# Query loads by head pair, scatters through disjoint views, and gathers issued ahead of scatters, in a fused retention and mixture-of-experts kernel

## The chip, the cores and the metric

The kernel runs on one core of a Trainium2 chip. The metric is the device time of one execution in microseconds, as a median of several runs. The trace behind all rows is one profiled execution of the same kernel.

## The reference

The inputs q, k and v have 8 batches, 8 heads, 576 positions and 64 values a head. The first half is retention: scores with a causal, exponentially decaying mask and no softmax. The second half is a switch layer over the 4608 rows that come out: each row goes to the one of 8 experts with the largest logit and is scaled by its gate.

```python
scores = scale * np.matmul(q, k.transpose(0, 1, 3, 2))
Dmat = np.where(rel >= 0, gamma[:, None, None] ** rel[None, :, :], 0.0)
x = np.matmul(scores * Dmat[None], v)        # then (B * S, H * D) = (4608, 512)

logits = x @ w_gate                          # 8 experts
expert_idx = np.argmax(logits, axis=1)
for e in range(E):
    mask = expert_idx == e
    h = np.maximum(x[mask] @ w1[e], 0.0)     # 512 -> 1024
    out[mask] = gate_w[mask, None] * (h @ w2[e])
```

## The kernel before, in words

Every engine runs its instructions in the order in which the program writes them; no planner reorders them. Waits between engines and DMAs are set from the tiles, and from the regions of DRAM tensors, that instructions share.

**Attention stage.** The sequence is cut into 40 blocks, five for each batch: four of 128 positions and a last one that holds the remaining 64 queries and 64 keys. The loop over blocks (i, or batch b and block c) does for each: GpSimd scales one head pair of the next batch's queries (`scale_q`, line 219, tile qq from qt) and the keys of block i + 3 (`scale_k`, line 229, kk from kt); TensorE makes scores, transposes keys (psk, copied to kT), updates the state, transposes the block's result back to rows (psr, written to the DRAM tensor `x_rows`), forms the output (psx) and at the end of the block transposes the scaled query pair (`stage_TQ`, psq, copied to qT by ScalarE). SP issues the loads: keys and values of block i + 7, from seven buffers each, the write of `x_rows`, and in block 4 of batch b the whole query of batch b + 2 as one DMA of 1 MB (`load_q`, line 93), into one of two buffers. The four head pairs of batch 0 come as four DMAs at the start, and batch 1 after the first blocks. From block 21 on one 512 KB piece of expert weights is loaded in each block (wst, three staging buffers) and cast to bf16 by VectorE. Routing runs beside the later batches on VectorE.

**Expert stage.** The rows of each expert come in two units: two tiles of 128 rows (phase 0, routed from the first half of the tokens) and three tiles (phase 1). `seq` lists the sixteen units: phase 0 of experts 0 to 2, phase 1 of the same, and then both phases of each expert from 3 on. For a unit `mm1` multiplies by w1 (pm, ReLU on ScalarE into ht), `trans` transposes the gathered rows of the next unit (pt from xg, copied to xt by VectorE), and `mm2` multiplies by w2 (py), scales by the gate on VectorE (ys, four buffers) and scatters the tile to `out` with an indirect DMA of GpSimd (line 755). `gather` (line 603) fetches a unit's rows into xg (six buffers) with one indirect DMA of GpSimd for each tile. The weights of experts 2 to 7 are 48 pieces of 512 KB over six staging buffers: each cast, up to five on VectorE within `mm1` and one on ScalarE after each tile of `mm2`, is followed by the load of another piece.

The gathers of the first three units are issued during the last blocks of attention, and those of units 4 and 5 when the third unit is done, since their slots are known only then. From the fourth unit on the loop issues the gather of unit i + 2 at its end, behind the scatters of unit i:

```python
            if nxt:
                trans(*nxt)
            mm2(e, ph, ht, during2)
        if i >= 3 and i + 2 < len(seq):
            gather(*seq[i + 2])
```

After the last unit a count of overflowing rows is read by all engines (line 814), and a branch (line 816) skips a fallback that nothing here needs.

Of the kernel before, what the change touches and what calls it, by code (L numbers as in the profile page):

```python
# [3 lines left out]

# [9 lines left out]
F32 = mybir.dt.float32  # L14
# [4 lines left out]
P = 128  # L19
B, H, S, DH = 8, 8, 576, 64  # L20
DM = H * DH
E, F = 8, 1024
NP = H // 2
NCH = 4
# [7 lines left out]
CA = 256  # L32
CB = 384
# [5 lines left out]
def kernel(  # L39
# [10 lines left out]
    nc = tc.nc  # L50
# [22 lines left out]
    ldq = p1.enter_context(tc.tile_pool(name="ldq", bufs=2))  # L73
# [11 lines left out]
    NB = len(blocks)  # L85
    qts, kts, vts, qrs = {}, {}, {}, {}

    def load_q(b, first):

        qt = ldq.tile([P, H, NCH, DH], F32, tag="q", name="qt")  # L90
        step = 2 if first else H
        for h in range(0, H, step):
            nc.sync.dma_start(out=qt[:, h:h + step, :, :],
                              in_=q[b, h:h + step, 0:NCH * P, :].rearrange("h (p s) d -> p h s d", p=P))
        qts[b] = qt

    def load_k(i):

        b, c = blocks[i]
        kt = ldk.tile([P, H, DH], F32, tag="k", name="kt")  # L100
        if c < NCH:
            nc.sync.dma_start(out=kt[:, :, :], in_=k[b, :, c * P:(c + 1) * P, :].rearrange("h p d -> p h d"))
        else:
            nc.sync.dma_start(out=kt[0:REM, :, :], in_=q[b, :, NCH * P:S, :].rearrange("h p d -> p h d"))
            nc.sync.dma_start(out=kt[REM:P, :, :], in_=k[b, :, NCH * P:S, :].rearrange("h p d -> p h d"))
        kts[i] = kt

    def load_v(i):

        b, c = blocks[i]  # L110
        vt = ldk.tile([P, H, DH], F32, tag="v", name="vt")
        if c < NCH:
            nc.sync.dma_start(out=vt[:, :, :], in_=v[b, :, c * P:(c + 1) * P, :].rearrange("h p d -> p h d"))
        else:
            for j in range(2):
                nc.sync.dma_start(out=vt[j * REM:(j + 1) * REM, 0:NP, :],
                                  in_=v[b, NP * j:NP * (j + 1), NCH * P:S, :].rearrange("h p d -> p h d"))
        vts[i] = vt

    load_k(0)  # L120
    load_q(0, True)
    load_v(0)
    for i in range(1, 5):
        load_k(i)
        load_v(i)


    ident = consts.tile([P, P], F32, name="ident")
# [73 lines left out]
    def cast_w(eng):  # L202
        e, part, st = staged.pop(0)
        w1b, w2b = wb[e]
        c = part % 4
        if part < 4:
            casts[eng](out=w1b[:, c, :], in_=st[:, :])
        else:
            casts[eng](out=w2b[:, 2 * c:2 * c + 2, :], in_=st[:, :].rearrange("p (s d) -> p s d", d=DM))
# [6 lines left out]
    def scale_q(b, p):  # L216
        h0 = 2 * p
        qq = wkp.tile([P, NCH, P], F32, tag="qq")
        nc.gpsimd.tensor_tensor(  # L219
            out=qq[:, :, :].rearrange("p s (h d) -> p h s d", d=DH), in0=qts[b][:, h0:h0 + 2, :, :],  # L220
            in1=qg[:, 0:NCH, h0:h0 + 2].rearrange("p s h -> p h s").unsqueeze(3)
                .to_broadcast([P, 2, NCH, DH]), op=ALU.mult)
        qqs[(b, p)] = qq

    def scale_k(i):
        if i >= NB:
            return
        kk = wk3.tile([P, H, DH], F32, tag="kk")
        nc.gpsimd.tensor_tensor(out=kk[:, :, :], in0=kts.pop(i)[:, :, :],  # L229
                                in1=kg[:, blocks[i][1], :].unsqueeze(2).to_broadcast([P, H, DH]), op=ALU.mult)  # L230
        kks[i] = kk
# [365 lines left out]
    def gather(e, ph):  # L597
        nb = (CA if ph == 0 else CB) // P
        nr = NTOK // 2 if ph == 0 else NTOK
        for j in range(nb):  # L600
            i = j * E + e
            xg = gp.tile([P, DM], BF16, tag="xg", name="xg")
            nc.gpsimd.indirect_dma_start(  # L603
                out=xg[:, :], out_offset=None, in_=x_rows[0:nr, :],
                in_offset=bass.IndirectOffsetOnAxis(ap=slots[ph][1][:, i:i + 1], axis=0),
                bounds_check=nr - 1, oob_is_err=False)
            gat_t[(e, ph, j)] = xg
# [30 lines left out]
    stage_TK(1)  # L638
    stage_SC(0)
    stage_S(0)  # L640
    load_q(1, False)
    load_k(5)
    load_v(5)
    load_k(6)
# [6 lines left out]
    for i, (b, c) in enumerate(blocks):  # L651
        if c < NP and b + 1 < B:
            scale_q(b + 1, c)
        scale_k(i + 3)
        stage_SC(i + 1)
        stage_TK(i + 2)
        stage_S(i + 1)
        if i > 0:
            stage_R(i - 1)
        if c == 0 and b > 0:  # L660
            stage_L1(b - 1)
        stage_AV(i)
        if i + 7 < NB:
            load_k(i + 7)
            load_v(i + 7)
        if c == 4 and b + 2 < B:
            load_q(b + 2, False)
        if c < NP and b + 1 < B:
            stage_TQ(b + 1, c)
        if c == 0 and b > 0:  # L670
            stage_L2(b - 1)
        if i >= first_early and nearly < len(early):
            load_w(*early[nearly], stpool)
            nearly += 1
        if len(staged) > 2 or (i == NB - 1):
            while len(staged) > (2 if i < NB - 1 else 0):
                cast_w("V")
        if (b, c) == (B // 2, 1):
            rf = route_first()
        if rf is not None:  # L680
            steps(rf, 5)
        if i == NB - 5:
            while steps(rf, 1):
                pass
            gather(0, 0)
            gather(1, 0)
            gather(2, 0)
# [16 lines left out]
    psH = p2.enter_context(tc.tile_pool(name="psH", bufs=3, space=PSUM))  # L704
    psY = p2.enter_context(tc.tile_pool(name="psY", bufs=3, space=PSUM))

    seq = [(e, 0) for e in range(3)] + [(e, 1) for e in range(3)] + [(e, ph) for e in range(3, E) for ph in (0, 1)]
    xts = {}
    wq = [(e, i) for e in range(2, E) for i in range(8)]
# [6 lines left out]
    def trans(e, ph):  # L716
        nb = (CA if ph == 0 else CB) // P
        xt = xtp.tile([P, NPT, nb * P], BF16, tag=f"xt{ph}", name="xt")
        for j in range(nb):
            xg = gat_t.pop((e, ph, j))  # L720
            pt = psT.tile([P, NPT, P], BF16, tag="pt")
            for c in range(NPT):
                tr(pt[:, c, :], xg[:, c * P:(c + 1) * P], identb[:, :])
            nc.vector.tensor_copy(out=xt[:, :, j * P:(j + 1) * P], in_=pt[:, :, :])  # L724
        xts[(e, ph)] = xt
# [18 lines left out]
    def mm2(e, ph, ht, between):  # L744
        nb = (CA if ph == 0 else CB) // P
        w1b, w2b = wb[e]
        tids, tidg, gat = slots[ph]
        for j in range(nb):
            i = j * E + e
            py = psY.tile([P, DM], F32, tag="py")  # L750
            for fb in range(NFB):
                mm(py[:, :], ht[:, fb, j * P:(j + 1) * P], w2b[:, fb, :], fb == 0, fb == NFB - 1)
            ys = yp.tile([P, DM], F32, tag="ys")
            nc.vector.tensor_scalar(out=ys[:, :], in0=py[:, :], scalar1=gat[:, i:i + 1], scalar2=None, op0=ALU.mult)  # L754
            nc.gpsimd.indirect_dma_start(  # L755
                out=out[:, :], out_offset=bass.IndirectOffsetOnAxis(ap=tids[:, i:i + 1], axis=0),
                in_=ys[:, :], in_offset=None, bounds_check=NTOK - 1, oob_is_err=False)
            between()

# [12 lines left out]
    for i, (e, ph) in enumerate(seq):  # L772
        nxt = seq[i + 1] if i + 1 < len(seq) else None
        quota = [5]

        def during1():
            if i < 3:
                steps(rr, 6)
            if i >= 1 and quota[0] > 0 and staged and (i >= 2 or len(staged) > 2):
                cast_w("V")  # L780
                fetch(1)
                quota[0] -= 1

        def during2():
            if i < 3:
                steps(rr, 8)
            if staged:
                cast_w("A")
                fetch(1)

        ht = mm1(e, ph, during1)
        if nxt == (0, 1):
            mm2(e, ph, ht, during2)
            while steps(rr, 1):
                pass
            gather(0, 1)
            gather(1, 1)
            trans(*nxt)
        else:
            if nxt:  # L800
                trans(*nxt)
            mm2(e, ph, ht, during2)
        if i >= 3 and i + 2 < len(seq):
            gather(*seq[i + 2])
    p2.close()


# [8 lines left out]
    with tc.If(over > 0):  # L816
        with ExitStack() as p3:
# [24 lines left out]
            for e in range(E):  # L842
# [4 lines left out]
                with tc.For_i(0, NT, 1) as t:  # L847
# [8 lines left out]
                        out=xg[:, :], out_offset=None, in_=x_rows[:, :],  # L856
# [16 lines left out]
                    for fb in range(NFB):  # L873
# [5 lines left out]
                        out=out[:, :], out_offset=bass.IndirectOffsetOnAxis(ap=ci[:, 0:1], axis=0),  # L879
                        in_=ys[:, :], in_offset=None, bounds_check=NTOK - 1, oob_is_err=False)  # L880
# [30 lines left out]
```

## Time and profile before

| | us |
|---|---|
| median of 3 runs | 565.05 |
| lowest and highest run | 563.92, 566.07 |
| profiled execution | 561.75 |
| its span | 560.0 |

| engine | busy us | share of the span |
|---|---|---|
| TensorE, matmuls | 384.8 | 69% |
| TensorE, weight loads | 267.3 | 48% |
| VectorE | 200.6 | 36% |
| ScalarE | 162.9 | 29% |
| GpSimd | 162.7 | 29% |

The span is what the profiler saw from the first to the last instruction; the execution's own time holds 1.75 us more. The mean granted clock of TensorE was 0.841 of full speed. Attention takes the first 265 us or so, the experts the rest. A share of busy time is a mean over both stages, so the stages have to be looked at one by one.

### The profile page before, as it was taken

The page shows a single profiled execution, that of the slowest core. Times are in us where ns is not written, and L with a number is a line of the kernel's source. Part 1 is how long each engine was busy: PE and PEld are TensorE (multiplying, and loading weights), DVE is VectorE, ACT ScalarE, POOL GpSimd, SP SyncE. Part 2 cuts the span into 40 slices and gives each one's busy share as a digit, 9 for nine tenths or more (in the row PEclk, how much of TensorE's full clock was granted, in tenths as well). Part 3 has the DMA queues.
Part 4 walks back from the last instruction along what each step waited for, and adds up shares of the span by engine and source line. Part 5 has one row for each costly group of instructions (what it writes and reads, how often), then busy time and mean ns, then how long its engine had stood idle before and what let it go on. Part 6 is the DMA issues. An engine that isn't in the chain of part 4 may idle for free. (4 is left out here: it accounts for less than half of the span.)

```text
span 560.0 us, 14566 instructions
## 1 busy us (share of the span) xinstructions
PE 384.8 (69%) x6322; PEld 267.3 (48%) x6322; DVE 200.6 (36%) x453; ACT 162.9 (29%) x301; POOL 162.7 (29%) x196
## 2 busy tenths in 40 slices
PE   4695959779696758795684491935786848677660
PEld 3584848567575647674462250413443434344330
DVE  2342323323275755764892340403321211112110
ACT  3252524335251422342332162313210212121020
POOL 8423305060514206240021512124213232422220
PEclk9898998979797997889798596858877878888695
DMA  8956483736488595561768497276111111111110
GB/s 212 231 135 167 99 204 77 194 78 164 116 221 241 127 274 143 156 180 50 266 240 336 137 319 287 94 275 220 57 47 54 58 56 57 67 57 47 61 60 14
DMA packets 112010, 82.33 MB, mean 147 GB/s; under 512 B 83263, under 2 KB 96063, under 8 KB 111937
## 3 DMA queue, kind: packets, MB, share of 16 engines
q1 hardware_dynamic: 106816, 66.61, 41.6%
q0 software_dynamic: 5120, 14.69, 7.6%
q8 instruction: 52, 0.85, 0.7%
q14 instruction: 22, 0.17, 0.1%
HBM read 67.13 MB, written 15.20 MB: 147 GB/s over the span
## 5 line engine op out<-in xcount | busy, mean ns | idle before, releaser
L740 ACT ACTIVATE ht<-pm 128x384 bf16<-128x384 f32 (+1 forms) x96 | 50.5, 526 | 202.7 <-PE pm L57 202.1
L755 POOL DMA_INDIRECT out_dram<-ys,tids x40 | 40.8, 1019 | 216.7 <-DVE ys L754 107.0
L57 PE MATMUL py<-w2b,ht 128*128 128x512 bf16 x320 | 91.1, 452 | 0.0
L57 PE MATMUL pm<-xt,w1b 128*128 128x256 bf16 (+1 forms) x512 | 75.2, 306 | 7.3 <-DVE xt L724 7.3
L60 PE MATMUL pt<-identb,xg 128*128 128x128 bf16 x160 | 20.8, 279 | 83.6 <-DMA xg<-x_rows,tidg 83.0
L219 POOL TENSOR_TENSOR qq<-qt,qg 128x512 f32<-128x512 f32 x32 | 33.8, 1060 | 137.1 <-DMA qt<-in_q_dram 96.1
L57 PEld LDWEIGHTS <-w1b 128*128 128x128 bf16 x512 | 51.1, 100 | 30.9 <-issue 9.6
L724 DVE COPY xt<-pt 128x512 bf16<-128x512 bf16 x40 | 16.6, 422 | 125.6 <-PE pt L60 125.5
L57 PEld LDWEIGHTS <-ht 128*128 128x128 bf16 x320 | 36.2, 115 | 48.6 <-issue 25.4
L60 PEld LDWEIGHTS <-xg 128*128 128x128 bf16 x160 | 12.7, 120 | 92.7 <-DMA xg<-x_rows,tidg 91.6
L754 DVE TENSOR_SCALAR ys<-py,gat 128x512 f32<-128x512 f32 x40 | 30.0, 750 | 65.5 <-PE py L57 65.4
L60 PE MATMUL psq<-ident,qq 128*128 128x128 f32 x128 | 25.6, 335 | 40.5 <-POOL qq L219 40.5
L229 POOL TENSOR_TENSOR kk<-kt,kg 128x512 f32<-128x512 f32 x40 | 43.4, 1092 | 18.5 <-issue 11.6
L603 POOL DMA_INDIRECT xg<-x_rows,tidg x40 | 41.2, 1030 | 12.1 <-issue 9.6
L360 DVE TENSOR_TENSOR xT<-psx,xo 128x512 f32<-128x512 f32 x32 | 22.1, 692 | 51.4 <-ACT xo L352 51.4
L60 PEld LDWEIGHTS psq<-ident,qq 128*128 128x128 f32 x128 | 16.4, 165 | 44.2 <-POOL qq L219 42.8
L60 PE MATMUL psk<-ident,kk 128*128 128x128 f32 x160 | 30.9, 323 | 9.3 <-POOL kk L229 7.0
L251 ACT COPY kT<-psk 128x512 f32<-128x512 f32 x40 | 23.6, 590 | 39.5 <-PE psk L60 39.5
L57 PE MATMUL psx<-qT,so 64*64 64x64 f32 x512 | 32.7, 221 | 1.7 <-issue 1.7
L241 ACT COPY qT<-psq 128x512 f32<-128x512 f32 x32 | 18.9, 590 | 45.5 <-PE psq L60 45.5
L311 DVE TENSOR_TENSOR sc<-pssc,tri 128x512 f32<-128x512 f32 (+1 forms) x40 | 25.2, 630 | 19.0 <-PE pssc L57 19.0
L352 ACT COPY xo<-psx 128x512 f32<-128x512 f32 (+1 forms) x40 | 21.8, 546 | 33.2 <-PE psx L57 33.0
(119 smaller groups left out, 527.4 us busy)
## 6 DMA issues: line engine op xcount, KB each, us to landing
wst<-in_moe_w_dram SPq DMA_DIRECT2D x64, 512.0 KB, 6.2
kt<-in_k_dram SPq DMA_DIRECT2D x32, 256.0 KB, 4.4
vt<-in_v_dram SPq DMA_DIRECT2D x32, 256.0 KB, 4.6
qt<-in_q_dram SPq DMA_DIRECT2D x7, 1024.0 KB, 7.6
x_rows<-xr SPq DMA_DIRECT2D x32, 128.0 KB, 2.4
qt<-in_q_dram SPq DMA_DIRECT2D x4, 256.0 KB, 4.7
kt<-in_q_dram SPq DMA_DIRECT2D x8, 128.0 KB, 2.9
kt<-in_k_dram SPq DMA_DIRECT2D x8, 128.0 KB, 3.1
```

The costliest lines, as they stand in the source:

```text
L57: nc.tensor.matmul(out=out, lhsT=lhsT, rhs=rhs, start=start, stop=stop, skip_group_check=True)
L60: nc.tensor.transpose(out=out, in_=in_, identity=identity)
L219: nc.gpsimd.tensor_tensor(out=qq[:, :, :].rearrange("p s (h d) -> p h s d", d=DH), in0=qts[b][:, h0:h0 + 2, :, :], in1=qg[:, 0:NCH, h0:h0 ...
L229: nc.gpsimd.tensor_tensor(out=kk[:, :, :], in0=kts.pop(i)[:, :, :], in1=kg[:, blocks[i][1], :].unsqueeze(2).to_broadcast([P, H, DH]), op=A ...
L251: nc.scalar.copy(out=kT[:, :, :].rearrange("p a t -> p (a t)"), in_=pst[:, :])
L311: nc.vector.tensor_tensor(out=sc[:, :, 0:n, :], in0=ps[:, :, 0:n * DH].rearrange("p j (a i) -> p j a i", i=DH), in1=tri[:, :].unsqueeze(1) ...
L352: nc.scalar.copy(out=xo[:, :], in_=psx[:, 1, 0:n * P])
L360: nc.vector.tensor_tensor(out=dst, in0=psx[:, 0, 0:n * P], in1=xo[:, :], op=ALU.add)
L603: nc.gpsimd.indirect_dma_start(out=xg[:, :], out_offset=None, in_=x_rows[0:nr, :], in_offset=bass.IndirectOffsetOnAxis(ap=slots[ph][1][:, ...
L740: nc.scalar.activation(out=ht[:, f0:f0 + per, :], in_=pm[:, :, :], func=AF.Relu)
L754: nc.vector.tensor_scalar(out=ys[:, :], in0=py[:, :], scalar1=gat[:, i:i + 1], scalar2=None, op0=ALU.mult)
L755: nc.gpsimd.indirect_dma_start(out=out[:, :], out_offset=bass.IndirectOffsetOnAxis(ap=tids[:, i:i + 1], axis=0), in_=ys[:, :], in_offset=N ...
```

## The change

`load_q` loads one head pair (256 KB) at a time. Batch 1 is loaded in between the first keys and values, and in block c (0 to 3) of batch b the pair c of batch b + 2 is loaded; the load in block 4 is gone. The scatters write through 40 views of `out` that the tracking of dependencies takes as disjoint, one for each scatter. The gather of unit i + 2 is issued between `trans` of unit i + 1 and `mm2` of unit i; the branch for the third unit is as it was, and the gathers of units 4 and 5 with it.

```diff
-    def load_q(b, first):
-
-        qt = ldq.tile([P, H, NCH, DH], F32, tag="q", name="qt")
-        step = 2 if first else H
-        for h in range(0, H, step):
-            nc.sync.dma_start(out=qt[:, h:h + step, :, :],
-                              in_=q[b, h:h + step, 0:NCH * P, :].rearrange("h (p s) d -> p h s d", p=P))
-        qts[b] = qt
+    def load_q(b, p):
+
+        if p == 0:
+            qts[b] = ldq.tile([P, H, NCH, DH], F32, tag="q", name="qt")
+        h = 2 * p
+        nc.sync.dma_start(out=qts[b][:, h:h + 2, :, :],
+                          in_=q[b, h:h + 2, 0:NCH * P, :].rearrange("h (p s) d -> p h s d", p=P))
...
     load_k(0)
-    load_q(0, True)
+    for p in range(NP):
+        load_q(0, p)
     load_v(0)
-    for i in range(1, 5):
+    load_k(1)
+    load_v(1)
+    load_q(1, 0)
+    for i in range(2, 5):
         load_k(i)
         load_v(i)
+        load_q(1, i - 1)
...
     stage_S(0)
-    load_q(1, False)
     load_k(5)
...
-        if c == 4 and b + 2 < B:
-            load_q(b + 2, False)
+        if c < NP and b + 2 < B:
+            load_q(b + 2, c)
...
+    outs = iter(bass_types.dram_disjoint_views(out, E * (CA + CB) // P))
...
             nc.gpsimd.indirect_dma_start(
-                out=out[:, :], out_offset=bass.IndirectOffsetOnAxis(ap=tids[:, i:i + 1], axis=0),
+                out=next(outs)[:, :], out_offset=bass.IndirectOffsetOnAxis(ap=tids[:, i:i + 1], axis=0),
...
             if nxt:
                 trans(*nxt)
+            if i >= 3 and i + 2 < len(seq):
+                gather(*seq[i + 2])
             mm2(e, ph, ht, during2)
-        if i >= 3 and i + 2 < len(seq):
-            gather(*seq[i + 2])
```

## Rows read from the trace of the kernel before

**Rows 1.** Waits of the span: who waited for whom, total us, times, longest.
```profile
PE psq L60 <- POOL qq L219: 40.5, 8, 7.1
PEld L60 <- DMA xg<-x_rows,tidg: 91.6, 30, 13.6
```

**Rows 2.** Timeline, TensorE: start us, us, line, operation, count, [idle before, releaser].
```profile
52.56 1.12 PE L60 MATMUL psq<-ident,qq 128*128 128x128 f32 x4 [5.64 <-POOL qq L219]
...
59.62 0.65 PE L60 MATMUL psq<-ident,qq 128*128 128x128 f32 x4
...
64.19 0.66 PE L60 MATMUL psq<-ident,qq 128*128 128x128 f32 x4
...
83.76 1.12 PE L60 MATMUL psq<-ident,qq 128*128 128x128 f32 x4 [6.59 <-POOL qq L219]
```

**Rows 3.** Timeline, SP's queue, around 45 us.
```profile
44.98 0.57 SPq L93 DMA_DIRECT2D qt<-in_q_dram  x1
```

**Rows 4.** Timeline, GpSimd, the same batch.
```profile
51.45 1.06 POOL L219 TENSOR_TENSOR qq<-qt,qg 128x512 f32<-128x512 f32 x1 [18.03 <-DMA qt<-in_q_dram]
```

**Rows 5.** Timeline, GpSimd, between two units of the expert stage.
```profile
415.90 1.00 POOL L755 DMA_INDIRECT out_dram<-ys,tids  x1 [2.58 <-DMA out_dram<-ys,tids]
419.41 0.98 POOL L755 DMA_INDIRECT out_dram<-ys,tids  x1 [2.51 <-issue]
420.69 1.04 POOL L603 DMA_INDIRECT xg<-x_rows,tidg  x1 [0.30 <-issue]
```

**Rows 6.** Timeline, TensorE, the same units.
```profile
415.36 3.66 PE L57 MATMUL pm<-xt,w1b 128*128 128x256 bf16 x32
...
423.58 0.61 PE L60 MATMUL pt<-identb,xg 128*128 128x128 bf16 x4 [4.57 <-DMA xg<-x_rows,tidg]
...
447.31 3.66 PE L57 MATMUL pm<-xt,w1b 128*128 128x256 bf16 x32
```

**Rows 7.** DMA issues: tensors, queue, count, KB each, median us to landing.
```profile
qt<-in_q_dram SPq DMA_DIRECT2D x7, 1024.0 KB, 7.6
qt<-in_q_dram SPq DMA_DIRECT2D x4, 256.0 KB, 4.7
```

**Rows 8.** Windows: stretch, length, busy per engine, granted clock, DMA share, GB/s.
```profile
51.50:82.60 31.10, 24.44 (x658) 20.38 (x658) 10.13 (x21) 11.98 (x23) 9.18 (x9) 0.88 0.58 141
175.40:210.20 34.80, 24.48 (x658) 20.09 (x658) 21.85 (x51) 11.33 (x23) 10.25 (x9) 0.89 0.75 199
```

**Rows 9.** Windows, a stretch of the expert stage.
```profile
320.00:340.00 20.00, 15.54 (x93) 8.49 (x91) 6.87 (x12) 12.99 (x21) 2.02 (x2) 0.98 0.95 333
```

**Rows 10.** Timeline, TensorE, third and fourth unit.
```profile
292.61 3.66 PE L57 MATMUL pm<-xt,w1b 128*128 128x256 bf16 x32
296.10 3.62 PE L57 MATMUL py<-w2b,ht 128*128 128x512 bf16 x16
...
317.40 6.93 PE L57 MATMUL pm<-xt,w1b 128*128 128x384 bf16 x32 [0.52 <-DVE xt L724]
324.17 0.61 PE L60 MATMUL pt<-identb,xg 128*128 128x128 bf16 x8
...
325.29 5.34 PE L57 MATMUL py<-w2b,ht 128*128 128x512 bf16 x24
...
330.47 5.36 PE L57 MATMUL pm<-xt,w1b 128*128 128x384 bf16 x32
```

**Rows 11.** Chain of waits that ended last: start us, us, what.
```profile
540.74 0.75 DVE ys L754
...
541.80 4.62 DMA out_dram<-ys,tids
```

**Rows 12.** Timeline, all engines, between third and fourth unit.
```profile
299.75 0.75 DVE L754 TENSOR_SCALAR ys<-py,gat 128x512 f32<-128x512 f32 x1 [0.97 <-PE py L57]
...
312.63 1.00 POOL L603 DMA_INDIRECT xg<-x_rows,tidg  x1 [0.30 <-issue]
```

**Rows 13.** The branch's line: operation, durations min/median/max in ns, first and last start.
```profile
L816 PEldq COMPARE_BRANCH  x1: 4076/4076/4076, 542.6 to 542.6; - x1
```

More of the change, by code (lines that the diff above doesn't have):

```diff
@@ L5 @@
 import concourse.bass as bass
+import concourse.bass_types as bass_types
 import concourse.tile as tile
```

## The prediction

> **What bounds the kernel now.** I read the waits of the whole span first, then the timelines of TensorE, SP and GpSimd around the longest of them, then busy time by stretch, then the chain that ended last. TensorE carries the work in both stages, and it stops for two things [rows 1]: 40.5 us in 8 waits for a scaled query tile (psq on qq), and 91.6 us in 30 waits for gathered rows (the weight load's row on xg). What each of them is late for, only the timelines say.
>
> In the attention stage the wait comes once per batch. The reader is to see in [rows 2] a transpose of psq at 52.56 after 5.64 us of idling, at 1.12 us for its four matmuls, and one at 59.62 that took 0.65 us after no wait: the second cost of a stall is a slow block behind it (52.56 to 59.62 is 7.06 us; 59.62 to 64.19, a block of the same kind, is 4.57). The cause stands in [rows 3] and [rows 4]: SP issues the 1 MB query load at 44.98, behind the value load that waits for the block before, and scaling starts at 51.45, as soon as it has landed. The load is issued when its user is next in line.
>
> In the expert stage [rows 5] show the chain. Scatters of one unit go out at 415.90 and 419.41, 3.5 us apart although one takes 1.0 us: each waits until the one before has landed. The gather for the next unit stands behind them at 420.69, and TensorE transposes its rows at 423.58, after 4.57 us of idling [rows 6]. A pair of units takes 415.36 to 447.31, 31.95 us.
>
> **The change, part by part.**
>
> *Query loads.* The 1 MB load per batch becomes four of 256 KB, one per block, each a full batch ahead of its scaling. Lead: five blocks, over 20 us at 4.57 each, against 4.7 us to land [rows 7]. The buffer is that of two batches before, whose last reader ran in the batch before, so SP is not held up by it. SP issues three more loads per batch; it waits for other engines during most of each batch and has room for them. Value: the 40.5 us go. The slow blocks go too: 7.06 less 4.57 less some 0.5 for two transposes of the router in it, 2.0 each; for seven stalls 13.5, the shorter ones costing a little less. Ceiling 54. Late next: the DMA engines. A batch without weights used 0.58 of 31.1 us, 18.0 us of transfers [rows 8], and would now have 31.2 - 6.6 - 2.0 = 22.6 us: 80 per cent. The batch with weights used 0.75 of 34.8, 26.1 us, and at 0.95, the highest share seen [rows 9], needs 27.5 us, where TensorE would need about 26. The loads run seven blocks ahead and smooth that, so I take off 4: **50 us**. Bounds: 0, if the engines were full, and 54. At the start the query pieces of batch 1 go ahead of later keys: each of 256 KB, some 1.3 us at the 199 GB/s of the second row there; the scaling of keys may start that much later, while the query that it waits beside comes earlier.
>
> A rule speaks against the split: the Trainium skill, DMA: Bandwidth & Descriptors, Rules for kernel authors, wants at least 1 MiB in a DMA, and its section on the anatomy of one DMA gives a fixed cost of about 2 us each. By that, 21 more transfers cost an estimated 42 us if nothing covers them, and the forecast below would be some 463. In the rows a 256 KB load takes 4.7 us and a 1 MB load 7.6, so a fixed part is there; what matters is whether it occupies the engines or is only latency, which is the second rival.
>
> *Scatters as disjoint views.* This takes away the wait of a scatter for the one before. No row shows a scatter without it. Nearest above: 3.5 us apart, as now. Nearest below: a gather, 1.0 us of GpSimd and 0.3 between two. I take 1.3, since 1.0 is what the scatter itself takes. What waits next is the ys tile, on four buffers. GpSimd then has ten such instructions per pair of units, 13 us, beside 19 us of TensorE.
>
> *Gathers ahead of scatters.* The gather for unit i+2 now stands before the scatters of unit i. Queued behind it on GpSimd are those scatters; who would wait for them is ys, then py, then TensorE. Its own wait is for a row buffer: six in rotation, units of two and three in turn, so it needs the transposes of unit i or earlier, which ran before the second products of unit i-1. It finds the buffer free, and its rows are there one unit early. The wait for xg goes to nothing from the fourth unit on.
>
> Units without a stall, from start to start [rows 10]: 256 columns 3.49, 384 columns 5.36 less 0.17 of overlap, 5.19; second products 3.46 for two tiles, 5.18 (325.29 to 330.47) for three; transposes of three tiles 1.12, of two 0.75. A unit of the first kind is 3.49 + 1.12 + 3.46 = 8.1, of the second 5.19 + 0.75 + 5.18 = 11.1. From the fourth unit to the sixteenth: 13.1 (317.40 to 330.47, cold start in it) + 11.5 + 11.1, then five of 8.1 and four of 11.1, and 10.4 for the last: 131 us. Before, the same ran from 317.40 to 540.74 [rows 10, 11], 223 us.
>
> Late next in this stretch are the expert weights. By the code 14 of 48 pieces are cast and 20 issued when the fourth unit starts, so 28 loads of 0.52 MB, 11 scatters of 0.26 MB and 10 gathers of 0.13 MB lie before the last cast: 18.9 MB. At the 333 GB/s of [rows 9] that is 57 us; casts refill the queue from about 311, so the last lands at 368. By TensorE alone it would be needed at 356. VectorE and ScalarE run casts in order with copies that TensorE needs, so TensorE stands there: **12 us** added (5 to 30, the upper end at 250 GB/s). Gain of the stretch 223 - 131 - 12 = **80 us**.
>
> *Before the fourth unit* the gathers stay behind the scatters in program order, but those are no longer in series. The last ys ends at 300.5, its scatter takes to 301.8, the third gather starts near 304.7 where it started at 312.63 [rows 12]: **8 us** earlier.
>
> *The tail.* The last scatter follows its ys (541.49) instead of the landing of the one before (541.80 + 4.62) [rows 11]: 4.9 us. Late next is the branch at the end, which on TensorE's sequencer lasts to 542.6 + 4.1 = 546.7 [rows 13]. I take **4** (0 to 5).
>
> **Sum.** 50 + 80 + 8 + 4 = 142 of the profiled execution's 561.75: 420. The median of the runs is 565.05, 0.6 per cent above that execution; about half of this goes with the stalls, so I put **421 us**. The likeliest case by itself reaches from 404 (54 + 92 + 8 + 5, rounded) to 442 (stage one at 38, weights at 22 over).
>
> **Rivals.**
>
> 1. *Scatters stay in series* (the views do not lift the wait; only the order changes). GpSimd then needs 5 x 3.5 + 5 x 1.3 = 24 us per pair, more than TensorE's 19: five pairs, 26 us, with the 8 and the 4 lost: 459. For it: nothing shows a free scatter. Against: the gathers, the same kind of instruction, follow each other at 1.3 us. 0.08.
>
> 2. *The attention stage becomes bound by the DMA engines.* If four small query loads occupy them as long as their times to land suggest, 4 x 4.7 - 7.6 = 11 us more, a batch needs 18 + 11 = 29 us of transfers, 30.5 at 0.95: nearly all of the 50 is lost, some 468. For it: the 4.7. Against: a time to land holds the wait behind other loads in the queue, and the bytes are the same. Through this the rule above would be right. 0.14.
>
> 3. *Slower: TensorE is granted the lower clock.* The price is in [rows 2]: 1.12 for 0.65, a factor of 1.7. On 7 x 22.6 us of attention that gives 38.4 per batch against 31.2 now, 50 us lost; on the 131 us of experts 223, no gain; with the tail and the fourth unit's start about 600. It decides when more than 0.7 of the 289 us run at that level (0.7 x 202 = 142). For it: the clock was low behind every stall. Against: in the one stretch of experts without a long stall it was granted 0.98 [rows 9]. 0.02.
>
> 4. *It does not do what it says*: waits stay where they were, 562 to 567. The semaphores would have to follow from something that the order of the code does not show. 0.02.
>
> **How the numbers follow.** 0.74 for the forecast, the rest as given. Range 403 to 460: the forecast's own and the first rival; left out are the second, third and fourth and a remainder. A difference under 0.5 per cent (2.8 us) can't be told from none. Slower by more: 0.02. Same: 0.01, half of the fourth rival. Faster: 0.97.
>
> **What would show it.** Query part: no psq wait over 1 us, batches of 22 to 24 us, DMA share near 0.8; wrong if share is 0.95 and psk or psq still wait. Scatters: starts 1.3 us after each other where ys allows, else 3.5. Gathers: no wait for xg after the fourth unit, pairs of 19 us; if a scatter waits behind a gather, the buffer count was wrong. Weights: casts that wait for wst in units five to eight. The forecast fails if pairs stay over 24 us or a batch over 28.

## The result and the profile after

The changed kernel takes 421.04 us (median of 4 runs, 416.44 to 422.42) against 565.28 for the kernel before (4 runs on the same chip): 0.744 of its time, 95% interval 0.737 to 0.750. The profiled execution took 416.44, the fastest of the four, with a span of 414.7 us, so the terms below, which are read from the profiled executions of both kernels, add up to 145.3 us, 1 us more than the medians differ by. A kernel's executions can fall into a fast and a slower state, and every ratio in this document is of the fast ones alone, so that a median over all runs can lie somewhat above its ratio.

The first lines of the page say how: busy time of each engine, its share of the span, its instructions.

```profile
span 414.7 us, 14606 instructions
...
PE 348.0 (84%) x6306; PEld 251.6 (61%) x6322; DVE 199.6 (48%) x453; ACT 163.1 (39%) x301; POOL 163.3 (39%) x196
...
PEclk9999999999999899999986989699989999999995
```

The other engines do what they did, in as many microseconds. TensorE's matmuls are the same ones (a few records are missing), yet take 348.0 us instead of 384.8, since the granted clock rose from a mean of 0.841 to 0.95. Up to 6 of these 37 us may be the missing records (16 of py at 0.389 us). By this estimate some 30 of the 145 us come from the clock, and the rest is idle time that went.

**Attention.** Timeline of TensorE, the transposes of the scaled queries of two batches (start, us, line, operation, count):

```profile
65.45 0.66 PE L61 MATMUL psq<-ident,qq 128*128 128x128 f32 x4
...
70.24 0.66 PE L61 MATMUL psq<-ident,qq 128*128 128x128 f32 x4
...
74.81 0.65 PE L61 MATMUL psq<-ident,qq 128*128 128x128 f32 x4
...
88.33 0.66 PE L61 MATMUL psq<-ident,qq 128*128 128x128 f32 x4
```

Against [rows 2] nothing stands in brackets: no idle time before any of them, 0.66 where the first of a batch took 1.12, and 22.9 us from batch to batch. The windows of this batch and of one with weights (engines' busy time, granted clock, DMA share, GB/s) answer to [rows 8]:

```profile
65.30:88.20 22.90, 22.52 (x664) 18.72 (x660) 9.95 (x21) 11.84 (x23) 9.37 (x9) 1.00 0.78 188
...
139.00:166.30 27.30, 22.91 (x662) 18.80 (x659) 21.32 (x51) 11.28 (x23) 9.87 (x9) 1.00 0.87 237
```

**Experts.** GpSimd's timeline: the first two scatters of the stage, then two gathers and the scatters of one unit of three tiles.

```profile
233.39 1.08 POOL L761 DMA_INDIRECT out_dram<-ys,tids  x1 [36.51 <-DVE rh L566]
234.78 1.00 POOL L761 DMA_INDIRECT out_dram<-ys,tids  x1 [0.32 <-DVE rh L566]
...
335.71 1.01 POOL L608 DMA_INDIRECT xg<-x_rows,tidg  x1 [0.30 <-issue]
337.02 0.99 POOL L608 DMA_INDIRECT xg<-x_rows,tidg  x1 [0.30 <-issue]
340.43 1.03 POOL L761 DMA_INDIRECT out_dram<-ys,tids  x1 [2.41 <-DVE ys L760]
342.16 1.00 POOL L761 DMA_INDIRECT out_dram<-ys,tids  x1 [0.70 <-DVE ys L760]
343.88 0.99 POOL L761 DMA_INDIRECT out_dram<-ys,tids  x1 [0.72 <-DVE ys L760]
```

The first two leave 1.39 us apart, so the second did not wait for the first to land. What it did wait for is its own ys, which VectorE finished at 234.50, 0.28 us before:

```profile
233.76 0.74 DVE L760 TENSOR_SCALAR ys<-py,gat 128x512 f32<-128x512 f32 x1
```

Later ones leave 1.73 us apart, again the pace at which ys comes; the gathers stand ahead of them. TensorE's units:

```profile
323.76 3.66 PE L58 MATMUL pm<-xt,w1b 128*128 128x256 bf16 x32
...
331.82 5.36 PE L58 MATMUL pm<-xt,w1b 128*128 128x384 bf16 x32
...
342.65 3.66 PE L58 MATMUL pm<-xt,w1b 128*128 128x256 bf16 x32
```

That is 8.06 and 10.83 us for the two kinds of unit, 18.89 for a pair that took 31.95 [rows 6]. What TensorE still waits for after attention (total us, times, longest), with the weight load's row on xg, to be set beside [rows 1], in front:

```profile
PEld L61 <- DMA xg<-x_rows,tidg: 9.0, 2, 8.6
PE pt L61 <- DMA xg<-x_rows,tidg: 8.1, 1, 8.1
PE pt L61 <- DVE xt L730: 6.1, 7, 4.3
PE pm L58 <- DVE xt L730: 5.5, 3, 4.8
```

Of the 30 waits for xg in [rows 1] the weight load's row keeps two, and the matmuls' row one, of 8.1 us: it comes before the fourth unit.

### The profile page after: what moved, and what is told of

It is laid out like the page before. It is cut to its first block, busy times and chain, and to the rows that moved or that the text cites. A ratio compares the mean times of both kernels' runs of the same rounds, so it can differ in the third digit from the quotient of the medians.

```text
span 414.7 us, 14606 instructions
## 1 busy us (share of the span) xinstructions
PE 348.0 (84%) x6306; PEld 251.6 (61%) x6322; DVE 199.6 (48%) x453; ACT 163.1 (39%) x301; POOL 163.3 (39%) x196
## 4 chain that ended last, share of the span: by engine, by line
PE 61%; DVE 10%; DMA 9%; issue 8%; ACT 4%; SPq 3%; POOL 2%; POOLq 0%; DVEq 0%; ACTq 0%
PE psx L58 12%; PE py L58 12%; PE pm L58 12%; DMA wst<-in_moe_w_dram 6%; PE psr L61 5%; PE psk L61 4%; PE pss L58 4%; PE pssc L58 4%; PE psl L58 3%; ACT xo L357 2%; PE psq L61 2%; DVE pay L556 2%; PE pt L61 1%; DVE xT L365 1%; POOL out_dram L761 1%
## 5 line engine op out<-in xcount | busy, mean ns | idle before, releaser
L58 PE MATMUL pm<-xt,w1b 128*128 128x256 bf16 (+1 forms) x512 | 76.5, 310 | 5.5 <-DVE xt L730 5.5
L58 PE MATMUL py<-w2b,ht 128*128 128x512 bf16 x304 | 71.4, 389 | 1.0 <-issue 0.2
L58 PEld LDWEIGHTS <-ht 128*128 128x128 bf16 x320 | 31.5, 100 | 36.3 <-issue 3.9
L730 DVE COPY xt<-pt 128x512 bf16<-128x512 bf16 x40 | 15.5, 419 | 42.9 <-PE pt L61 41.9
L61 PE MATMUL psk<-ident,kk 128*128 128x128 f32 x160 | 26.8, 290 | 9.6 <-POOL kk L234 7.3
L58 PEld LDWEIGHTS psx<-qT,so 64*64 64x64 f32 x512 | 28.1, 135 | 1.1 <-issue 1.0
L58 PE MATMUL pssc<-qT,kT 64*64 64x64 f32 x1024 | 24.6, 225 | 3.9 <-DVE sc L316 2.5
L282 ACT COPY so<-pss 128x256 f32<-128x256 f32 x32 | 11.9, 372 | 39.5 <-DVE so L281 31.1
L58 PE MATMUL psx<-sc,vt 64*64 64x64 f32 x1152 | 26.6, 227 | 0.4 <-issue 0.4
L58 PE MATMUL pss<-vt,kk 64*64 64x64 f32 x1024 | 23.4, 225 | 3.6 <-issue 3.6
```

What stands on the lines that cost most here:

```text
L58: nc.tensor.matmul(out=out, lhsT=lhsT, rhs=rhs, start=start, stop=stop, skip_group_check=True)
L61: nc.tensor.transpose(out=out, in_=in_, identity=identity)
```

## The experiments

Each has the changed kernel or the kernel before as its base; times are medians, with the ratio to the kernel before from the same chip. The diffs are against the changed kernel.

### One part undone

`no_q` has the query loads of the kernel before; `no_views` and `no_gather` are these edits:

```diff
 no_views
-                out=next(outs)[:, :],
+                out=out[:, :],
...
 no_gather
-            if i >= 3 and i + 2 < len(seq):
-                gather(*seq[i + 2])
             mm2(e, ph, ht, during2)
+        if i >= 3 and i + 2 < len(seq):
+            gather(*seq[i + 2])
```

> Views and early gathers, query loads as before. If the two stages add up, the attention stage ends at about 263 and the whole takes 421 + 47 = 468 us. If the faster expert stage owes something to a shorter attention stage (weights of the first experts, a state of queues), it would be 475 or more.

> Query loads and early gathers, but all scatters through the one output tensor. My theory, that the views lift the wait of a scatter for the one before: scatters 3.5 us apart, GpSimd needs 5 x 3.5 + 5 x 1.3 = 24 us per pair of units and becomes the bound, 421 + 26 + 8 + 4 less what the weights cost anyway: about 455 us. Rival, the order of gathers does it alone: 421 to 428 with the wait for xg gone.

> Query loads and views, gathers back at the end of a unit. My theory: after the last product of a unit come ys 0.75, its scatter 1.3, two or three gathers of 1.3 and 2.8 to land, against a first product of 3.5 or 5.2 us in between, so TensorE idles about 4 us before units of three tiles and 1 us before units of two: pairs of about 24 us, 421 + 22 = 443 us. Rival, the views do it alone: no wait for xg over 1 us and 421 to 425 us.

| kernel | us | ratio, 95% |
|---|---|---|
| no_q | 464.4 | 0.823 (0.818 to 0.828) |
| no_views | 446.3 | 0.789 (0.785 to 0.794) |
| no_gather | 465.9 | 0.825 (0.819 to 0.831) |

`no_q`: as expected within 4 us; the stages add up. `no_views` is dearer than the changed kernel by 25 us, so the views do lift a wait, but it was expected at 455. In the two traces it loses 7 us before the fourth unit (54.3 for 47.1), 15 from there to the last ys (150.4 for 135.8) and 7 in the tail (22.8 for 15.6); expected were 8, 26 less what the weights cost anyway, and 4. It is the middle that came out lower, and its GpSimd timeline shows why:

```profile
380.45 1.00 POOL L760 DMA_INDIRECT out_dram<-ys,tids  x1 [2.56 <-issue]
381.75 1.04 POOL L608 DMA_INDIRECT xg<-x_rows,tidg  x1 [0.30 <-PE py L58]
...
384.42 0.99 POOL L608 DMA_INDIRECT xg<-x_rows,tidg  x1 [0.30 <-PE pm L58]
385.71 1.03 POOL L760 DMA_INDIRECT out_dram<-ys,tids  x1 [0.30 <-issue]
389.28 1.00 POOL L760 DMA_INDIRECT out_dram<-ys,tids  x1 [2.54 <-DVE xt L729]
392.82 0.98 POOL L760 DMA_INDIRECT out_dram<-ys,tids  x1 [2.54 <-DVE ys L759]
394.10 1.04 POOL L608 DMA_INDIRECT xg<-x_rows,tidg  x1 [0.30 <-PE pm L58]
```

Scatters in series are 3.5 us apart, as I had it. But the 2.5 us in which a scatter waits for the one before are not lost where gathers stand between the two: after 384.42 the next scatter starts at once. I had added 5 x 3.5 and 5 x 1.3; of the five scatter waits of a pair two are covered, and this pair takes 19.9 us (376.86 to 396.76), not 24; on TensorE three pairs take 20.3 each.

`no_gather` was expected at 443 and takes 466. The idle time was right, its consequence not. TensorE there, before a unit of three tiles:

```profile
422.93 3.66 PE L58 MATMUL pm<-xt,w1b 128*128 128x256 bf16 x32
428.38 0.40 PE L61 MATMUL pt<-identb,xg 128*128 128x128 bf16 x4 [1.79 <-DMA xg<-x_rows,tidg]
429.74 0.61 PE L61 MATMUL pt<-identb,xg 128*128 128x128 bf16 x4 [0.95 <-DMA xg<-x_rows,tidg]
431.38 0.61 PE L61 MATMUL pt<-identb,xg 128*128 128x128 bf16 x4 [1.04 <-DMA xg<-x_rows,tidg]
431.79 5.68 PE L58 MATMUL py<-w2b,ht 128*128 128x512 bf16 x16
437.30 5.36 PE L58 MATMUL pm<-xt,w1b 128*128 128x384 bf16 x32
```

It idles 3.8 us in three pieces, near the 4 expected, but the transposes in between and the product behind run in part at the lower clock (a granted 0.62 from 428.3 to 437.3): 5.68 us for what took 3.62 in [rows 10]. The unit takes 14.4 us instead of 8.1, a pair 26.5 (343.50 to 422.93 for three). I had counted the wait and left out the clock. That explains pairs of 26.5 instead of 24, about half of the 23 us missed. The other half lies earlier: from the fourth to the ninth unit this trace takes 81.8 us for 60.5 in the changed kernel, with waits for xg of up to 5.5 us and slow products behind them; the expectation priced pairs only.

### One part alone

> Only the query loads are changed; scatters and gathers as before. My theory: the attention stage is bound by TensorE once the queries are early, so its end (the router's last transposes, 263.3 before) comes at about 216, and the whole takes 565 - 48 = 517 us, the expert stage being as long as before. Rival, the DMA engines bind the attention stage: its end stays above 250 and the whole above 550.

> Views alone; query loads and gathers as before. My theory: scatters leave as ys comes, but the gathers stay behind them, pairs of about 24 us instead of 32: 565 - 8 - 4 - 64 = about 490 us. Rival, that the wait for xg has the order as its only cause: 545 or more.

> Early gathers alone. My theory: no wait for xg from the fourth unit on, but scatters in series 3.5 us apart, so that GpSimd is the bound at 24 us per pair and TensorE waits for ys and py instead: about 500 us. Rival, that the order alone makes the gain of the expert stage: about 470 us with pairs of 19 us. Rival, that early gathers without views only put the scatters later: 550 or more.

| kernel | us | ratio, 95% |
|---|---|---|
| q_only | 522.2 | 0.924 (0.916 to 0.931) |
| views_only | 519.3 | 0.909 (0.902 to 0.915) |
| gather_only | 500.1 | 0.875 (0.868 to 0.882) |

`q_only`: attention ends at 218.0 (the router's last transposes) for 216 expected, and the whole gains 43 us; the DMA engines do not bind it. `views_only` was expected at 490 and misses for the reason of `no_gather`: pairs of 26.2 us. `gather_only` came as expected, though not as reasoned: its pairs take 20.2 us, not 24, and the stretch from the end of attention to the fourth unit stays as long as before, 53.3 us (54.1 in the kernel before, 47.1 in the changed one). The kernel before ran at 565.6 and 569.5 in the two sets, so gains are compared by the ratios, as shares of 565 us: alone they are 43, 52 and 71, and each taken last gives 45, 26 and 46. Queries are worth the same either way. Views and gathers are worth less beside each other: both take from the wait for xg, so in part each does the other's work.

### Earlier, or in pieces?

The query part moves the loads and cuts them up. Three kernels take these apart, from batch 2 on:

```diff
-        if c < NP and b + 2 < B:
-            load_q(b + 2, c)
 q_split_late
+        if c == 4 and b + 2 < B:
+            for p in range(NP):
+                load_q(b + 2, p)
 q_whole_early
+        if c == 0 and b + 2 < B:
+            load_q(b + 2, None)             # one DMA of 1 MB
 q_burst_early
+        if c == 0 and b + 2 < B:
+            for p in range(NP):
+                load_q(b + 2, p)
```

> As the changed kernel, but from batch 2 on the four loads of 256 KB are issued in block 4 of the batch, next to their use, as the one load was before. My theory, only being early counts: the first pair lands some 4.7 us after its issue instead of 6.5, so a stall of about 4 us and a slow block return in six batches: 421 + 6 x (4 + 2) = 457 us. Rival, the split is what helps (the first pair lands alone and fast): within 5 us of 421.

> As the changed kernel, but from batch 2 on the query is again one load of 1 MB, issued in block 0 of the batch before its user, four blocks earlier than before the change. My theory, only being early counts: within 3 us of 421. Rival, the split is needed or harmful (its fixed costs occupy the engines): faster by 10 us or more when whole; or, if a 1 MB burst delays keys and values, slower by 5 us or more with waits of kk for kt.

> As the changed kernel, but from batch 2 on the four loads of 256 KB are issued together in block 0 of the batch before their user. The whole 1 MB load in that place took 431 us. If the burst costs (1 MB in the queues at once, ahead of keys, values and of TensorE's own instructions), this takes about 431 too, with as much idle time of TensorE that nothing releases. If the size of one DMA costs, it takes about 421.

| kernel | us | ratio, 95% |
|---|---|---|
| changed kernel | 421.0 | 0.744 (0.737 to 0.750) |
| q_split_late | 446.0 | 0.782 (0.776 to 0.788) |
| q_whole_early | 431.1 | 0.754 (0.747 to 0.760) |
| q_burst_early | 424.0 | 0.745 (0.740 to 0.750) |

Being early is worth most: without it 22 to 25 of the 43 us are lost again, and the old wait is back (psq on qq, 21.3 us in 8 waits). The expected 457 put the stalls some 11 us too high. The split has a value of its own while the loads stay late: 464.4 us with one DMA (`no_q`, which also keeps the old load of batch 1) and 446.0 with four. Once they are early little of it is left. That the four together in one block run like the spread ones says that the burst does not cost, or no more than these runs can tell. One DMA of 1 MB, expected within 3 us of 421, is slower by 5 (by the ratios, against the burst) to 10 us (by the medians, against the changed kernel); its interval just overlaps that of the changed kernel, but its trace is clear of the others: attention ends at 231.9, against 220.9 with the burst and 213.8 to 219.2 in seven traces with the loads of the changed kernel. It is not the delay of keys that the expectation named for this case: kk waits for kt 4.8 us in 3 waits, as with the burst. Where part of the time goes is seen in its timeline:

```profile
75.42 0.56 PE L58 MATMUL pss<-vt,kk 64*64 64x64 f32 x20
...
78.47 0.69 PE L58 MATMUL pss<-vt,kk 64*64 64x64 f32 x12 [2.49 <-issue]
...
79.10 1.11 PE L61 MATMUL psr<-ident,xT 128*128 128x128 f32 x4
```

TensorE stops in the middle of a group of products for 2.49 us, waiting for nothing that the profile shows, and goes on at the lower level of the clock (a granted 0.88 over that batch). The query load was issued at 68.72, the DMA queue of the loads kept the engines 90.6 per cent busy from 75.0 to 78.5, and that window holds one packet of an instruction queue:

```profile
q1 hardware_dynamic: 2303, 0.78, 90.6%
q8 instruction: 1, 0.02, 1.6%
```

Such stops without a releaser are 13.6 us of TensorE's time before 235 us here, 8.3 in the changed kernel and 8.6 with the burst, so they are 5 of the 11 us that lie between this trace and that of the burst. A guess is that TensorE waits there for its own instructions, behind the query data. No run tested it, the packet alone says little (the windows just before and just after hold one too), and why 1 MB in one DMA would do it and four in a row would not stays open.

### Weights

```diff
-            nc.sync.dma_start(out=st[:, :], in_=moe_w1[e, c * P:(c + 1) * P, :])
+            n = F if e < 2 else F // 4
+            nc.sync.dma_start(out=st[:, 0:n], in_=moe_w1[e, c * P:(c + 1) * P, 0:n])
...
+        if e >= 2:
+            src = st[:, 0:F // 4].unsqueeze(1).to_broadcast([P, 4, F // 4])
...
```

> As the changed kernel, but for experts 2 to 7 only a quarter of each weight piece is loaded and the cast repeats it (most of the expert weights are left out; the number and size of casts and products stay). If the idle time in the seventh unit (4.3 us before the third transposes, casts behind it waiting for wst) is the DMA rate, it goes, with the casts' other waits: 6 us less, 415 us, and nothing else moves. If it is the casts themselves, nothing moves: 421 us.

It takes 414.1 us, 0.726 (0.720 to 0.733): 7 us less by the medians and 10 by the ratios, for 6 expected. In its trace the stretch that the weights bear on, from the fourth unit to the last ys, takes 130.7 us for 135.8, so 5 us are theirs. In the changed kernel, TensorE's timeline at the seventh unit:

```profile
302.63 0.61 PE L61 MATMUL pt<-identb,xg 128*128 128x128 bf16 x8
...
307.57 0.38 PE L61 MATMUL pt<-identb,xg 128*128 128x128 bf16 x4 [4.33 <-DVE xt L730]
```

VectorE's timeline at the same place shows what held the copies that the third transposes need:

```profile
304.14 0.69 DVE L212 CAST w1b<-wst 128x1024 bf16<-128x1024 f32 x1 [1.35 <-DMA wst<-in_moe_w_dram]
...
306.49 0.69 DVE L212 CAST w1b<-wst 128x1024 bf16<-128x1024 f32 x1 [1.66 <-DMA wst<-in_moe_w_dram]
307.10 1.32 DVE L730 COPY xt<-pt 128x512 bf16<-128x512 bf16 x3
```

They stand behind casts that wait for weights. With a quarter of the bytes the same place reads:

```profile
306.15 0.38 PE L61 MATMUL pt<-identb,xg 128*128 128x128 bf16 x4 [0.29 <-DVE xt L736]
```

### A faster version

The one long wait left, 8.1 us before the fourth unit, and the casts in the seventh:

```diff
 early45
         if nxt == (0, 1):
             mm2(e, ph, ht, during2)
-            while steps(rr, 1):
-                pass
-            gather(0, 1)
-            gather(1, 1)
             trans(*nxt)
         else:
             if nxt:
                 trans(*nxt)
+            if i == 1:
+                while steps(rr, 1):
+                    pass
+                gather(0, 1)
+                gather(1, 1)
...
 best: early45 and
-        quota = [5]
+        quota = [5 if i < 5 else 2]
```

> As the changed kernel, but the gathers of the fourth and fifth unit are issued in the second unit, before its second products, instead of after the third unit. If only their place behind the scatters of the third unit makes TensorE wait 8.1 us for xg there and start the fourth unit at the lower clock, both go: 10 us less, 411 us. If the rows came late for another reason (routing), the wait moves to the second unit and the time stays at 421.

> early45 and at most two casts instead of five on VectorE per unit from the sixth unit on, which are still in time for their experts. If casts that wait for weights hold back the copies that TensorE needs, the 4.3 us of the seventh unit go as well: some 5 us less than early45, 406 us. If the weights are needed earlier than I count, or the wait only moves, it takes as long as early45.

`early45` takes 412.4 us, 0.728 (0.724 to 0.732), and `best` 406.1, 0.719 (0.716 to 0.723). In `early45` the fourth unit starts without a wait for xg:

```profile
251.93 0.38 PE L61 MATMUL pt<-identb,xg 128*128 128x128 bf16 x4 [0.73 <-DVE xt L730]
...
252.82 5.36 PE L58 MATMUL pm<-xt,w1b 128*128 128x384 bf16 x32 [0.51 <-DVE xt L730]
```

The first products there take 5.36 us and not 6.9 or 7.4: the clock stayed up. Its GpSimd timeline also shows what a scatter costs when its ys has long been there, 1.33 us to the next (these two ys were done at 242.87 and 244.60):

```profile
248.33 1.03 POOL L761 DMA_INDIRECT out_dram<-ys,tids  x1 [0.30 <-issue]
249.66 1.00 POOL L761 DMA_INDIRECT out_dram<-ys,tids  x1 [0.31 <-issue]
```

In `best` the wait of the seventh unit is gone as well (0.29 at 301.33). One of 3.3 us is left in the fifth, which the changed kernel did not have (0.29 there) and `early45` has (2.7): the unit starts earlier, and VectorE's casts, one of them shown, wait for weights ahead of the copies:

```profile
277.94 0.69 DVE L212 CAST w1b<-wst 128x1024 bf16<-128x1024 f32 x1 [0.98 <-DMA wst<-in_moe_w_dram]
...
279.02 0.38 PE L61 MATMUL pt<-identb,xg 128*128 128x128 bf16 x4 [3.32 <-DVE xt L730]
...
301.33 0.38 PE L61 MATMUL pt<-identb,xg 128*128 128x128 bf16 x4 [0.29 <-DVE xt L730]
```

## Why the prediction was right, point by point

| term, us gained | predicted | by the two traces |
|---|---|---|
| attention, to the router's last transposes (263.33, 216.19) | 50 | 47.1 |
| from there to the fourth unit (54.07, 47.12) | 8 | 7.0 |
| fourth unit to the last ys (223.34, 135.78) | 80 | 87.6 |
| tail (19.26, 15.61) | 4 | 3.7 |
| sum | 142 | 145.3 |

*Query loads.* Right, and the ceiling of 54 with it. Batches without weights take 22.9 us for 22.6 expected at a DMA share of 0.78 for 0.80. The batch with weights came out at 27.3 for 27.5, but not for the reason given: the DMA share was 0.87, so the engines were not full. VectorE was busy for 21.3 of those 27.3 us with routing and casts beside its own part of attention, and TensorE waits for it and for ScalarE in small pieces, 3.4 us in all, as at 151.38 and 152.70; no run tested what the batch takes without the routing:

```profile
151.38 0.46 PE L58 MATMUL pssc<-kT 64*64 64x64 f32 x16 [0.93 <-DVE sc L316]
...
152.70 0.63 PE L61 MATMUL psk<-ident,kk 128*128 128x128 f32 x4 [0.85 <-ACT xr L380]
```

*The rule for large DMAs.* For bandwidth the Trainium skill (DMA: Bandwidth & Descriptors, Rules for kernel authors) wants DMAs of at least 1 MiB, and the prediction's estimate from that page was up to 42 us more, if nothing covers the fixed costs. Here the 28 quarters that replace seven loads are covered: TensorE's matmuls wait for scaled query tiles for 0.2 us in all. One whole load in the same place is not faster but some 5 to 10 us slower, so the measurement decides against the rule for this use. The second rival, through which the rule would have been right, falls with `q_only`.

*Scatters and gathers.* Scatters follow ys, 1.39 us apart at the closest; the 1.3 that I took for a free one is seen in `early45`, as 1.33. A pair takes 18.9 us for 19.2; no wait for xg above 0.4 us is left from the fifth unit on. The count of row buffers was right: no scatter waits behind a gather.

*Weights.* This is the term that was mis-sized: 12 us for what measures 4.8 (135.8 less the 131 without a stall) or 5.0 (less the 130.7 of `w_quarter`). It lies in the seventh unit, which took 13.8 us for 8.1: the 4.33 us shown and a slower product behind them. I divided by 333 GB/s at a share of 0.95 [rows 9], as if that were the ceiling. With the loads asked for faster, the engines gave more, over the whole stretch of the loads and over its best 20 us:

```profile
263.90:311.00 47.10, 41.98 (x248) 23.75 (x251) 23.31 (x39) 25.12 (x39) 19.41 (x19) 0.93 0.99 364
283.00:303.00 20.00, 19.89 (x129) 11.91 (x131) 10.67 (x17) 11.64 (x18) 10.68 (x10) 1.00 1.03 393
```

18.9 MB at 364 GB/s is 52 us and not 57, 5 of the 7 us by which the term was too high; what the other 2 are is not shown. The stall was in the seventh of the units five to eight, for the reason given, and `w_quarter` and `best` show that reason by taking it away in two ways.

*First rival.* Its mechanism is real (`no_views`), its price was too high by half, 25 us for 38, for the overlap of gathers with the wait of a scatter. *Third:* the granted clock rose instead of falling. *Fourth:* it falls too, since each part was seen to do what it says.

The 421 of the forecast is hit more closely than its terms deserve, which is luck. Attention, 3 us too good, and weights, 7 too bad, cancel in part and leave the sum 3.3 us too small. The forecast then added some 1 us for the median's lying above the profiled execution; it lies 4.6 above it, which makes up for those 3.3.

## What to carry to other kernels

Where an in-order engine issues both the stores of one step and the loads of the next, put the loads first and see that stores which can't overlap are known as such; either alone left pairs of 20 to 26 us here, both gave 19. Price a wait on TensorE with the slow stretch behind it: 3.8 us of idle time in three pieces left the product that followed at 5.68 us for 3.62, so the unit lost 6.3. When a load is late, issue it earlier first, and then cut it into the pieces that its users take: here the cut was worth some 18 us with the loads late and 5 to 10 with the loads early.

## What the runs showed of the hardware

The DMA engines moved 393 GB/s over 20 us at a share of 1.03, against the 333 at 0.95 that the kernel before showed; a share near one in a slow trace was not the ceiling. The other surprise is TensorE's stop of 2.49 us without a releaser, in the middle of a group, some 7 us after the issue of a 1 MB load and with the DMA engines busy; its cause is open.
